# A long convolution by FFT and a gated causal unit on one core: second half in order of n, new evictions, and written-out queues

## The chip, the core and the metric

The kernel runs on one core of a Trainium2 chip. The core's engines run side by side, each with its own in-order queue, and meet at semaphores. PE is TensorE (matmuls; PEld its weight loads), DVE is VectorE, ACT is ScalarE, POOL is GpSimd and SP is SyncE, which here only issues DMA transfers. SBUF is the working memory of 128 partitions. PSUM takes the matmuls' results: eight banks of 512 float32 values per partition, used here as four tiles of two banks. The metric is the device time of one execution in microseconds.

## The reference

Input x is 8 batches of 3200 positions (n) by 256 channels in float32. Each batch is filtered along the positions by a complex filter, channel by channel, and then goes through a gated unit with a causal convolution of five taps:

```
X = np.fft.rfft(x, axis=1)
Y = X * (filt_r + 1j * filt_i)[None, :, :]
y = np.fft.irfft(Y, n=3200, axis=1)
gate_pre[n] = sum(conv_w[k] * y[n - 4 + k] for k in range(5))    # zeros before n = 0
out = (sigmoid(gate_pre) * (y @ w_val)) @ w_out
```

## The kernel before

**The transform.** A position is written n = 32a + r, with a from 0 to 99 and r from 0 to 31. Eight chunks of a batch hold four values of r each, with a on the partitions. Per batch the work is this, with the helper and its line:

1. `load_x` (L161, POOL): a chunk of x comes in as bfloat16. `s1` (L417, PE): a transform over a by one matrix of cosines and sines. `so` (L408 on ACT or L410 on DVE): eviction from PSUM.
2. `turn` (L436, DVE): four transposes of 32x32 blocks put r on the partitions (tile tt).
3. `s2` (L446, PE): the transform over r, 13 frequency slots in seven groups u. `xs`: eviction. `zed` (L464, DVE): two products, with the filter's real part (za) and imaginary part (zb). `inva` (L477, PE): the inverse over r. `ue`: eviction to u.
4. `wr` (L498) and `lv` (L508, L509, both SP): u goes to a scratch tensor in DRAM (escr) and comes back as vt, with the frequency on the partitions. `ib` (L518, PE): the inverse over a, in eight chunks. `ye` (L528, ACT): scaled eviction into yt, the filtered signal of a batch. Its columns are ordered by r, then a.

**The gated unit**, eight chunks of four r (400 columns) per batch, channels on the partitions: `halo` (L535, L537, POOL) fills the four columns ahead of r = 0. `conv` (L545, PE): five taps as 64x64 diagonal matrices; four matmuls, of two row groups and two column groups, belong to each tap, and each row group r writes PSUM bank r. `gate` (L554, ACT): sigmoid. `val` (L563, PE): y times w_val. `gv` (L573, DVE): their product. `outp` (L583, PE): times w_out, eight matmuls for four groups of 100 positions. `oe`: eviction to o. `store` (L597, L598, SP): two DMAs, of 96 and of 4 partitions.

**The start.** POOL generates index tables, issues batch 0's eight chunks of x and then 32 transfers of the two filters (L222, L225, L228), which fill half of the partitions of fr_t and fi_t. SP copies them to the other half by eight DMAs (L253). DVE and ACT compute the transform tables.

**What sets the order.** A planner (`Plan`, L30) holds every step as a task with its engine or engines, an assumed cost, its dependences and the buffers that it takes and gives back. It keeps a clock per engine, and among the tasks that could start it takes the one of the lowest rank, a number written for each task from its batch and its step. The result is the order in which each engine's queue is issued. Copies from PSUM may go to ACT or DVE, whichever the planner finds. Buffers: four PSUM tiles, ten chunks of x, one so, two tt, four u, four vt, two yt, three o.

Of the kernel before, what the change touches and what calls it, by code (L numbers as in the profile page):

```python
# [8 lines left out]
FP32 = mybir.dt.float32  # L9
# [7 lines left out]
L = 100  # L17
# [3 lines left out]
NV = 4 * NS  # L21
RC = 4
NCH = R // RC
UCH = [(m, min(2, NM - m)) for m in range(0, NM, 2)]
ICH = [NCH - 1] + list(range(NCH - 1))
MAGIC = 12582912.0


class Plan:
# [3 lines left out]
    def __init__(self, room, stay=1.0):  # L33
        self.tasks, self.room, self.stay = {}, dict(room), stay

    def add(self, name, engines, rank, deps, emit, take=(), give=(), land=0.0, mode=None):
        self.tasks[name] = dict(engines=engines, rank=rank, deps=deps, emit=emit, take=take,
                                give=give, land=land, mode=mode)

    def run(self):  # L40
        left = dict(self.tasks)
        users, need = {}, {}
        for n, t in left.items():
            need[n] = len(t["deps"])
            for d in t["deps"]:
                users.setdefault(d, []).append(n)
        ready_at = {n: 0.0 for n in left}
        free = {}
        mode = None
        gives = []  # L50
        ready = {n for n in left if need[n] == 0}
        order = []
        now = 0.0
        while left:
            gives.sort()
            while gives and gives[0][0] <= now + 1e-9:
                for pool in gives.pop(0)[1]:
                    self.room[pool] += 1
            best = None
            for n in ready:  # L60
                t = left[n]
                if ready_at[n] > now + 1e-9:
                    continue
                if any(self.room[p] < 1 for p in t["take"]):
                    continue
                for e, cost in t["engines"].items():
                    if free.get(e, 0.0) <= now + 1e-9:
                        away = e == "PE" and t["mode"] != mode
                        key = (t["rank"] + (self.stay if away else 0.0), cost)
                        if best is None or key < best[0]:  # L70
                            best = (key, n, e, cost)
            if best is None:
                later = [ready_at[n] for n in ready if ready_at[n] > now + 1e-9]
                later += [v for v in free.values() if v > now + 1e-9]
                later += [g[0] for g in gives if g[0] > now + 1e-9]
# [665 lines left out]
```

## Time and profile before

| | |
|---|---|
| median of 3 runs | 348.83 us (344.46 to 350.54) |
| the profiled execution's own time | 346.47 us |
| its span, first to last instruction | 344.8 us |
| busy: PE, DVE, ACT, POOL | 288.3, 256.4, 267.8, 68.0 us |
| mean granted TensorE clock | 0.97 |
| moved by DMA | 70.91 MB, mean 206 GB/s |

The profile is of one execution. The table of busy time gives each engine's busy time, its share of the span and the number of its instructions. The slices cut the span into 40 parts of 8.6 us; a digit is the busy share in tenths. The groups are instructions of one line, engine and shape. The chain of waits follows the work that ended last back to its releasers. A matmul's duration contains its way through the array, so the step from one start to the next is the better price of a matmul in a dense stretch.

### The profile page before, as it was taken

The page shows a single profiled execution, that of the slowest core. Times are in us where ns is not written, and L with a number is a line of the kernel's source. Part 1 is how long each engine was busy: PE and PEld are TensorE (multiplying, and loading weights), DVE is VectorE, ACT ScalarE, POOL GpSimd, SP SyncE. Part 2 cuts the span into 40 slices and gives each one's busy share as a digit, 9 for nine tenths or more (in the row PEclk, how much of TensorE's full clock was granted, in tenths as well). Part 3 has the DMA queues.
Part 4 walks back from the last instruction along what each step waited for, and adds up shares of the span by engine and source line. Part 5 has one row for each costly group of instructions (what it writes and reads, how often), then busy time and mean ns, then how long its engine had stood idle before and what let it go on. Part 6 is the DMA issues. An engine that isn't in the chain of part 4 may idle for free.

```text
span 344.8 us, 9785 instructions
## 1 busy us (share of the span) xinstructions
PE 288.3 (84%) x3988; PEld 191.6 (56%) x3988; DVE 256.4 (74%) x340; ACT 267.8 (78%) x309; POOL 68.0 (20%) x142
## 2 busy tenths in 40 slices
PE   2634677639999987999779997999999999999992
PEld 0023031326667755776457764776577677766762
DVE  4985477938698996889849994989798999734541
ACT  3954286928898987898849986998999789887663
POOL 8687455210112112110211011100100000001000
PEclk9999999969999999899989998999999999999997
DMA  6999999995899989898869969795677568778544
GB/s 95 155 168 163 213 192 195 206 238 168 199 232 247 272 233 231 245 229 251 170 200 207 271 176 250 214 245 171 199 208 221 156 204 261 234 214 248 160 144 143
DMA packets 57421, 70.91 MB, mean 206 GB/s; under 512 B 8608, under 2 KB 37152, under 8 KB 57376
## 3 DMA queue, kind: packets, MB, share of 16 engines
q1 hardware_dynamic: 45344, 55.20, 53.4%
q0 software_dynamic: 12032, 15.08, 29.0%
q8 instruction: 31, 0.51, 0.6%
q14 instruction: 14, 0.11, 0.1%
HBM read 43.78 MB, written 39.85 MB: 243 GB/s over the span
## 4 chain that ended last, share of the span: by engine, by line
PE 43%; DMA 24%; DVE 15%; ACT 7%; issue 4%; POOL 4%; SPq 1%; ACTq 0%; POOLq 0%; DVEq 0%
DMA vt<-escr 13%; PE ps L583 12%; PE ps L545 10%; DMA xt<-in_x_dram 6%; PE ps L563 6%; DVE tt L436 5%; DVE gv L573 5%; PE ps L417 5%; PE ps L518 5%; PE ps L477 4%; DMA fi_t<-in_filt_i_dram 3%; PE ps L446 3%; ACT o L408 2%; DVE xs L410 2%; POOL xt L161 2%
## 5 line engine op out<-in xcount | busy, mean ns | idle before, releaser
L573 DVE TENSOR_TENSOR gv<-ps,gt 128x800 bf16<-128x800 f32 x64 | 62.7, 980 | 19.9 <-PE ps L563 13.6
L408 ACT ACTIVATE o<-ps 100x1024 f32<-100x1024 f32 x59 | 61.0, 1035 | 16.9 <-PE ps L583 12.9
L410 DVE CAST xs<-ps 128x1024 bf16<-128x1024 f32 (+1 forms) x44 | 50.4, 1145 | 29.0 <-PE ps L446 29.0
L583 PE MATMUL ps<-wo_t,gv 128*100 128x256 bf16 x512 | 68.7, 278 | 2.7 <-DVE gv L573 1.1
L545 PE MATMUL ps<-yt,dg_t 64*64 64x400 bf16 x1280 | 67.3, 339 | 0.3
L408 ACT ACTIVATE so<-ps 128x1024 bf16<-128x1024 f32 x53 | 54.5, 1029 | 15.9 <-PE ps L417 11.1
L528 ACT ACTIVATE yt<-ps 128x800 bf16<-128x800 f32 x64 | 53.9, 846 | 15.9 <-PE ps L518 15.7
L583 PEld LDWEIGHTS <-gv 128*100 128x100 bf16 x512 | 54.5, 125 | 18.6 <-DVE gv L573 9.0
L161 POOL DMA_DIRECT2D xt<-in_x_dram x64 | 35.4, 556 | 124.5 <-PE ps L417 119.8
L554 ACT ACTIVATE gt<-ps 128x800 bf16<-128x800 f32 x64 | 54.1, 847 | 6.5 <-PE ps L545 5.3
L417 PE MATMUL ps<-xt,cf_t 100*128 100x512 bf16 x128 | 47.5, 462 | 12.2 <-DMA xt<-in_x_dram 11.2
L563 PE MATMUL ps<-yt,wv_t 128*128 128x400 bf16 x256 | 54.4, 335 | 0.5 <-ACT gt L554 0.5
L408 ACT ACTIVATE u<-ps 128x1024 bf16<-128x1024 f32 (+1 forms) x46 | 44.9, 982 | 7.2 <-PE ps L477 6.6
L518 PE MATMUL ps<-ci_t,vt 104*128 104x100 f16 x512 | 34.3, 212 | 16.5 <-DMA vt<-escr 16.4
L518 PEld LDWEIGHTS <-vt 104*128 104x128 bf16 x512 | 29.6, 100 | 30.1 <-DMA vt<-escr 19.8
L545 PEld LDWEIGHTS <-dg_t 64*64 64x64 bf16 x1280 | 34.5, 108 | 17.3 <-issue 4.2
L436 DVE STREAM_TRANSPOSE tt<-so 128x1024 f32<-128x1024 f32 x32 | 40.6, 1272 | 3.2 <-ACT so L408 3.2
L464 DVE TENSOR_TENSOR za<-xs,fr_t 128x1024 bf16<-128x1024 bf16 (+1 forms) x56 | 36.1, 649 | 1.4 <-ACT xs L408 0.2
L464 DVE TENSOR_TENSOR zb<-xs,fi_t 128x1024 bf16<-128x1024 bf16 (+1 forms) x56 | 35.5, 640 | 1.4 <-DMA fi_t<-in_filt_i_dram 1.4
L477 PE MATMUL ps<-zb,b_t 64*64 64x256 bf16 x416 | 29.7, 294 | 4.4 <-DVE zb L464 4.4
L477 PE MATMUL ps<-za,a_t 64*64 64x256 bf16 x416 | 30.3, 298 | 2.4 <-DVE za L464 2.1
L446 PE MATMUL ps<-tt,w_t 64*64 64x256 bf16 x416 | 24.2, 305 | 9.0 <-DVE tt L436 4.4
(93 smaller groups left out, 181.9 us busy)
## 6 DMA issues: line engine op xcount, KB each, us to landing
out_dram<-o SPq DMA_DIRECT2D x64, 384.0 KB
xt<-in_x_dram POOLq DMA_DIRECT2D x64, 200.0 KB, 6.7
escr<-u SPq DMA_DIRECT2D x48, 256.0 KB
vt<-escr SPq DMA_DIRECT2D x64, 192.0 KB
escr<-u SPq DMA_DIRECT2D x8, 128.0 KB
vt<-escr SPq DMA_DIRECT2D x64, 16.0 KB
out_dram<-o SPq DMA_DIRECT2D x64, 16.0 KB
fr_t<-in_filt_r_dram POOLq DMA_DIRECT2D x8, 56.0 KB, 4.7
```

The costliest lines, as they stand in the source:

```text
L408: nc.scalar.activation(dst, src, AF.Copy, **kw)
L410: nc.vector.tensor_copy(dst, src)
L417: nc.tensor.matmul(ps[:, 512 * h:512 * h + 512], lhsT=cf_t[0:L].rearrange("p h c i -> p (h c i)"), rhs=xv[:, DQ // 2 * h:DQ // 2 * h + DQ ...
L436: nc.vector.transpose(dst, src)
L464: (nc.vector if e == "DVE" else nc.gpsimd).tensor_tensor(z[:, :, 0:nm * D], xs_[:, :, 0:nm * D], f[:, :, m0:m0 + nm, :].rearrange("p h m d ...
L477: nc.tensor.matmul(ps[64 * h:64 * h + 64, 512 * t + D * a:512 * t + D * a + D], lhsT=tab[rows, h, m0 + a, :], rhs=zz[w][rows, h, D * a:D * ...
L518: nc.tensor.matmul(ps[:, o:o + L], lhsT=v[0:NV, a, 128 * dh:128 * dh + 128], rhs=ci_t[0:NV, :], start=True, stop=True)
L545: nc.tensor.matmul(ps[64 * dh:64 * dh + 64, 512 * r:512 * r + RC * L], lhsT=dg_t[rows, dh, k, :], rhs=y[rows, dh, RC * j + k:RC * j + k + ...
L554: nc.scalar.activation(g[...], ps[:, :].rearrange("p (h n) -> p h n", h=2)[:, :, 0:RC * L], AF.Sigmoid)
L563: nc.tensor.matmul(ps[:, 512 * eh:512 * eh + RC * L], lhsT=wv_t[:, dh, 128 * eh:128 * eh + 128], rhs=y[:, dh, H + RC * j:H + RC * j + RC, ...
L573: nc.vector.tensor_tensor(gv_[...], ps[:, :].rearrange("p (h n) -> p h n", h=2)[:, :, 0:RC * L], g[...], op=ALU.mult)
L583: nc.tensor.matmul(ps[0:L, D * a:D * a + D], lhsT=gv_[:, eh, L * a:L * a + L], rhs=wo_t[:, eh, :], start=(eh == 0), stop=(eh == 1))
```

## The change

- **Order of n.** `ye` writes yt in order of n: it reads a chunk from PSUM with r and a exchanged and writes runs of four values. The gated unit then works on seven blocks of consecutive positions: six of 512 and one of 128. A block's conv waits for all eight chunks of its batch. `halo` is one memset. `outp` takes groups of 128 positions; so that each partition holds four consecutive rows of the output, `gv` reads its inputs at every fourth column and writes them in groups. `store` is one DMA of 128 partitions, except for the last full block, whose gv, oe and store are split in two.
- **Convolution.** Its matmuls write bank dh for channel half dh, from both row groups. In batches 6 and 7 two blocks of 512 are computed together by 32x32 tiles, 80 matmuls for the pair, in two PSUM tiles; the channels come out rotated, so w_val and w_out are held with rotated copies.
- **Filters.** One tile f_t holds both parts. POOL issues 24 transfers in place of 32, and eight copies on DVE (seven) and ACT (one) fill the other half in place of SP's eight DMAs. `zed` is one product of both parts in place of two.
- **Batch 0** has no way through DRAM: `pad` clears the rest of u, and `back` transposes u into vt on DVE in four pieces. A second inverse matrix (ci_t) fits its order of rows.
- **Buffers.** One tt, one u (a whole batch), one vt (a whole batch), four o. PSUM is one tile of four slots, and the plan names each task's slot.
- **Queues.** The order of each engine is a list of task numbers in the kernel; the planner only runs it to find slots and the order between engines. `warm` fills gaps that the planner sees on PE between 14 and 45 us with matmuls whose results nobody reads.
- **Smaller edits.** The taps' diagonal matrices are made by ACT in ten instructions, and w_val and w_out come in two steps.

The core of the diff:

```diff
-    NVB, NGB, NOB = 4, 3, 3
+TURN = (0,)
+SMALL = (6, 7)
...
+            for e, line in lines.items():
+                if line and free.get(e, 0.0) <= now + 1e-9 and can(line[0]):
+                    begin(line.pop(0), e)
...
+    ps_all = pp.tile([128, 4, 1024], FP32, name="ps")
...
-                    for h in range(2):
-                        nc.gpsimd.dma_start(
-                            out=dst[p:p + 16, h, m0:m1, :].rearrange("p m d -> p (m d)"),
-                            in_=fsrc(f, k + NS * h, [[100 * D, 16], [1, nm * D]]))
+                    nc.gpsimd.dma_start(
+                        out=dst[p:p + 16, :, m0:m1, :].rearrange("p h m d -> p h (m d)"),
+                        in_=fsrc(f, k, [[100 * D, 16], [NS * D, 2], [1, nm * D]]))
...
-        for m0, m1 in FCUT:
-            for dst in (fr_t, fi_t):
-                for t in range(2):
-                    p = 64 * t
-                    nc.sync.dma_start(out=dst[p + 32:p + 64, :, m0:m1, :],
-                                      in_=dst[p:p + 32, :, m0:m1, :])
...
+    def warm(us):
+        flat = w_t[...].rearrange("p s k -> p (s k)")
+        ps = psum()
+        for h in range(int(us / WARM)):
+            o = 512 * (h % 2)
+            nc.tensor.matmul(ps[:, o:o + 512], lhsT=flat[:, 0:128],
+                             rhs=flat[:, o + 128:o + 640], start=True, stop=True)
...
+    def twin(half, w, t, e):
+        m0, m1 = FCUT[half]
+        p = 64 * t
+        copy(e, f_t[p + 32:p + 64, w, :, m0:m1, :], f_t[p:p + 32, w, :, m0:m1, :])
...
+    def zed(b, u):
...
+        nc.vector.tensor_tensor(
+            z[:, :, :, 0:nm * D],
+            st.pop(("XS", b, u))[:, :, 0:nm * D].unsqueeze(1)
+            .to_broadcast((128, 2, 2, nm * D)),
+            f_t[:, :, :, m0:m0 + nm, :].rearrange("p w h m d -> p w h (m d)"), op=ALU.mult)
...
+    def pad(b):
+        st["U", b] = upool.tile([128, 32, D], BF16, name="u")
+        if b in TURN:
+            nc.gpsimd.memset(st["U", b][:, NS:32, :], 0.0)
...
+    def back(b, q):
+        if q == 0:
+            st["V", b] = vpool.tile([128, R, D], BF16, name="vt")
+        src, dst = (t_[:, :, DQ * q:DQ * q + DQ].bitcast(FP32).rearrange("p s w -> p w s")
+                    for t_ in (st["U", b], st["V", b]))
+        nc.vector.transpose(dst, src)
...
-            y[:, :, p0:p0 + RC, :].rearrange("p h a n -> p h (a n)"),
-            ps[:, :].rearrange("p (h n) -> p h n", h=2)[:, :, 0:RC * L],
+            y[:, :, H:H + N].rearrange("p h (a r) -> p h a r", r=R)[:, :, :, RC * j:RC * j + RC],
+            ps[:, :].rearrange("p (h n) -> p h n", h=2)[:, :, 0:RC * L]
+            .rearrange("p h (r a) -> p h a r", r=RC),
...
+        if not pair(b, c):
+            ps = psum()
+            for k in range(K):
+                for r, dh in ((0, 0), (1, 0), (0, 1), (1, 1)):
+                    rows = slice(64 * r, 64 * r + 64)
+                    o = 64 * (r ^ dh)
+                    nc.tensor.matmul(ps[o:o + 64, 512 * dh:512 * dh + w],
+                                     lhsT=dg_t[rows, dh, k, :],
+                                     rhs=y[rows, dh, BLK * c + k:BLK * c + k + w],
+                                     start=(k == 0), stop=(k == K - 1))
+            st["cv", b, c] = ps
+            return
+        two = [psum(0), psum(1)]
+        for k in range(K):
+            for n in range(4):
+                dh, s = n // 2, n % 2
+                p = BLK * (c + s) + k
+                for i in range(4):
+                    rows = slice(32 * i, 32 * i + 32)
+                    o = 32 * ((i + n) % 4)
+                    nc.tensor.matmul(two[s][o:o + 32, 512 * dh:512 * dh + BLK],
+                                     lhsT=dg_t[rows, dh, k, 32 * (i % 2):32 * (i % 2) + 32],
+                                     rhs=y[rows, dh, p:p + BLK],
+                                     start=(k == 0), stop=(k == K - 1))
...
-            for r, dh in ((0, 0), (1, 1), (0, 1), (1, 0)):
-                rows = slice(64 * r, 64 * r + 64)
-                nc.tensor.matmul(ps[64 * dh:64 * dh + 64, 512 * r:512 * r + RC * L],
...
+        if w == BLK:
+            o = o.rearrange("p h (r q) -> p h r q", r=RC)
+            i0, i1 = (t_.rearrange("p h (q r) -> p h r q", r=RC) for t_ in (i0, i1))
...
-                nc.tensor.matmul(ps[0:L, D * a:D * a + D],
-                                 lhsT=gv_[:, eh, L * a:L * a + L], rhs=wo_t[:, eh, :],
+                nc.tensor.matmul(ps[:, D * a:D * a + D],
+                                 lhsT=gv_[:, eh, 128 * a:128 * a + 128], rhs=wo_t[:, c % 2 * pair(b, c), eh, :],
...
-    plan = Plan(dict(ps=4, xt=NXT, so=1, t=2, xs=3, za=3, zb=3, u=4, e=2, v=NVB, y=2, g=NGB,
-                     gv=NGB, o=NOB))
+    plan = Plan(dict(xt=NXT, so=1, t=1, xs=3, z=3, u=1, e=2, v=1, y=2, g=NGB, gv=NGB, o=NOB), 4, QUEUES)
...
+                if slots and COLD[0] < idle and at < COLD[1] and at - idle > WARM:
+                    warm(at - idle)
```

610 lines of the change are left out of this document (344 added, 266 removed), and 70 rows, old and new, of tables (ACT, DVE, PE, POOL).

## The prediction, made before the changed kernel had run

> **What bounds the kernel now.** I read the busy table and the forty slices first, then the busy time by stage, then the chain that ended last for the weak stage, then the timeline of TensorE (PE) for the prices of a dense stage.
>
> ```profile
> PE 288.3 (84%) x3988; PEld 191.6 (56%) x3988; DVE 256.4 (74%) x340; ACT 267.8 (78%) x309; POOL 68.0 (20%) x142
> PE   2634677639999987999779997999999999999992
> DMA  6999999995899989898869969795677568778544
> ```
>
> No engine is far from full, and PE stands at 9 from slice 9 (78 us) almost to the end. The loss lies before it.
>
> ```profile
> 0.00:45.00 45.00, 22.49 (x178) 8.15 (x178) 30.47 (x81) 24.14 (x28) 31.36 (x69) 1.00 0.95 160
> 45.00:78.00 33.00, 20.72 (x244) 9.99 (x242) 21.89 (x29) 21.38 (x25) 12.18 (x23) 0.90 1.04 210
> 78.00:220.00 142.00, 129.68 (x1886) 90.90 (x1879) 115.06 (x130) 119.77 (x140) 20.40 (x41) 0.96 0.87 222
> 220.00:330.00 110.00, 106.94 (x1604) 77.01 (x1603) 85.06 (x98) 95.88 (x112) 4.02 (x10) 1.00 0.73 211
> ```
>
> Busy time by stage: columns PE, weight loads, DVE, ACT, POOL, then granted clock, DMA share, GB/s. Up to 78 us only 420 of 3988 matmuls run, while DMA is full. Much of that PE time is slow work: the first-stage matmul has these durations from 30 to 60 us, and from 220 us on.
>
> ```profile
> L417 PE MATMUL ps<-xt,cf_t x26: 606/628/632, 35.5 to 59.8; 100*128 100x512 bf16 x26
> L417 PE MATMUL ps<-xt,cf_t x22: 382/384/395, 221.1 to 264.0; 100*128 100x512 bf16 x22
> ```
>
> The recorded clock says 1.00 in both places, but two such matmuls step by 1.03 us early and by 0.45 late, so PE ran at half rate. The chain shows what the first batch waited for (start, us, what):
>
> ```profile
> 34.36 11.60 DMA xt<-in_x_dram
> ...
> 63.07 11.63 DMA vt<-escr
> ...
> 74.75 0.85 PE ps L518 x8
> ```
>
> PE's in-order queue held batch 0's inverse behind batch 1's input, and then the reload through DRAM came in at 74.7 us. The second stage needs a PE price list. In the timeline (start, us) the steps between starts are 0.91 for a projection of eight matmuls (L583), 0.68 for val (L563), 0.45 for one inverse chunk (L518), 0.97 for a conv block (L545).
>
> ```profile
> 301.59 0.52 PE L518 MATMUL ps<-ci_t,vt 104*128 104x100 f16 x8
> 302.04 1.04 PE L545 MATMUL ps<-yt,dg_t 64*64 64x400 bf16 x20
> 303.01 1.08 PE L583 MATMUL ps<-wo_t,gv 128*100 128x256 bf16 x8
> 303.92 0.84 PE L563 MATMUL ps<-yt,wv_t 128*128 128x400 bf16 x4
> 304.60 0.52 PE L518 MATMUL ps<-ci_t,vt 104*128 104x100 f16 x8
> ```
>
> With 0.45 for L417's pair, 0.15 for a frequency slot of L446 and 0.26 for one of L477, the whole program is 64x0.91 + 64x0.68 + 64x0.97 + 64x0.45 + 64x0.45 + 104x0.41 = 264 us. By 78 us, 48 matmuls of L417, 104 of L446, 200 of L477 and 16 of L518 had run: 22 us of it. The other 242 took 264 us (78 to 342): a fill of **0.92**; 2.8 us of last store follow.
>
> **The change, part by part.**
>
> *PE in the dense stage.* Rows in order of n give 25 groups of 128 per batch in place of 32 of 100: 400 projection matmuls in place of 512, 50x0.91 = 45.5 against 58.2, so -12.7. Val streams the same columns: 48x0.87 + 8x0.22 = 43.5, no change. Conv: 0.97 is five passes of 400 columns (0.17 each, val's rate) and 0.12 beside them. At 512 columns that is 5x0.218 + 0.12 = 1.21, 36 times; the 128-column rest 0.39, 8 times. No row has 32x32 tiles. A pair of blocks costs between 1.21 (sixteen tiles in one pass, as L545's four are) and 2.42 (nothing gained). Sixteen weight loads per pass weigh on it: L335 at half rate shows four in 0.107 us, so up to 0.43 for sixteen against 0.218. I take 1.4, nearer to L545's row, six times. Conv is then 43.6 + 3.1 + 8.4 = 55.1 against 62.1, -7.0. Odd offsets of the moving operand have no row; bounds none to a doubled pass, none taken, since every aligned row here streams at the column rate. PE needs 264 - 20 = **244 us**.
>
> *ACT and DVE.* By start-to-start steps (0.92 to 0.94 for 1024 columns on ACT, 1.14 on DVE, 0.72 for 800 on ACT, 0.90 on DVE) I count from the two lists of instructions: ACT 257 before and 253 after, DVE 249 and 249. Sixteen fewer evictions of o (64 to 48, and 8 small) give 12, one product of 2048 columns in place of two of 1024 (1.13 to 1.21 against 1.21) gives 3, fewer gates 1. The filter copies cost it back: seven on DVE, one on ACT. The nearest rows are 0.60 for 1024 and 1.03 for 1664 columns, so 0.5 to 1.6 each for 3072 to 3584; I take 0.9 on DVE, 3 on ACT. The back-transposes cost 4 steps of 1.16 (tt's row) to twice that, since words lie 512 B apart; I take 1.7. So these engines gain nothing, and at 231 us of PE after the start they need about 220 and 210: the cover is thin.
>
> Two operations lose their contiguous rows. gv reads PSUM and the gate at every fourth element, and yt is written in runs of four with PSUM read 100 words apart. The nearest rows are gv's 980 ns for 800 contiguous columns, and tt, whose words stand two apart, 1272 ns for 1024: both about 1.2 ns per column. So I take gv at 0.90 + 224x1.04 = 1.13 a step, with twice that as upper end (+54 us of DVE).
> The Trainium skill, Vector Engine (DVE) Microarchitecture Reference, section 5.2, speaks against this part: a source that hops at every element is given 1.73 to 2.5 ns per column, against 1.05 for pairs of adjacent words. It measured that in SBUF on 4-byte words; tt's row moves single words at full speed but only two words apart, so no run here decides it. By the page gv would be 1.8 to 2.6 us, +32 to +69 us of DVE, and the end about 317 to 357 us.
>
> *The start.* POOL issues 24 filter transfers in place of 32; the last one left at 28.7 and took up to 5.4. Eight issues of 0.51 are 4 us at most, none if the DMA engines (0.98 full there) are the limit: landing at 29 to 33. SP's eight duplicates go. Behind the last landing stand two copies (1.8), four products (4.6), an inverse slot pair and its eviction (1.5), four back-transposes (6.8). Batch 0's inverse starts at 44 to 48 instead of 74.7. The warming matmuls (at 14 to 45 us) use idle PE; where the plan's gap isn't there they cost up to 0.43 each and delay what stands behind them, a few us, but hold the rate that L417 lacked. I take **47 us** as start of the dense stage. Done by then: two batches of L417 (7.2), one of L446 and L477 (5.3): 12.5.
>
> *Buffers and queues.* tt, u and vt are single now. A batch's u must be written out before the next is filled; in a batch time of 31 us the chain u, DRAM, vt (12 us at 63 to 75) fits. Conv waits for all eight pieces of its batch, 8x0.72 on ACT; other batches' matmuls stand beside it in PE's queue. SP loses 56+8 second stores; POOL's halo copies (8 us) were off the path.
>
> *Sum.* (244 - 12.5) / 0.92 = 251.6; 47 + 251.6 + 2.8 = 301.4 span. What lies around the span is 346.47 - 344.8 = 1.7: 303.1, against the profiled execution's own 346.47. The median of the runs is 348.83, 1.007 of it: **305 us**.
>
> **Rivals.**
>
> *The transfers set the pace* (0.18). The kernel moves 70.9 MB; without batch 0's round trip (3.4) and the duplicates (1.7) 65.8, some 58 of them after 47 us. In 250 us that is 232 GB/s; the stages above gave 222 and 211. For it: PE and its weight loads waited 36 us for vt. Against: 30 us from 100 on ran at 247. At 222 GB/s the end is 47 + 262 + 4.5, 316 us on the median's scale; at 205 (the rate of 160 to 280) 338.
>
> *A fuller stage* (0.20). From 220 to 330 the fill by the same prices is 0.98; the two low stages of the clock come after idle vt waits. At 0.97: 47 + 239 + 4.5, 292; with a start at 44, 289. Against it: ACT and DVE need 0.9 all the way.
>
> *gv at twice a contiguous step* (0.05). DVE is the bound: 210 + 54 at 0.92, its share from 100 to 130, gives 47 + 287 + 4.5: 341 us. From about 1.6 us a step DVE is later than PE.
>
> *Row tiles in one bank take turns* (0.05), the case that ends slower. In L545 before, row group r writes bank r. After, both row groups write bank dh at once, four of them in a pair. If those can't overlap, a block needs a second pass (36x1.09 + 8x0.27) and a pair three more (6x3.3): +61 us of PE, 318 for the stage, 372 us. It is slower by 2% if over 46 of these 61 come. Against it: the partitions written are different ones.
> The Trainium skill, TensorEngine Tiling (Array Packing), Gotcha 1, has that rule: different row tiles cannot access the same PSUM bank simultaneously. No run so far shows a pass of this form.
>
> *It doesn't do what it says* (0.01): batch 0 still waits for DRAM; the two instruction lists show that its reload is gone.
>
> **How the numbers follow.** The forecast (295 to 316) has 0.51. Two per cent is about what can be told from no change here. Faster by over 2% (below 341.9) hold the forecast, the fuller stage, the transfers and half of gv: 0.91; the same 0.04; slower 0.05. The range 288 to 335 leaves out the row tiles, gv, and the ends of the fuller stage and of the transfers.
>
> **What would show it.** Right: first L518 near 45; 400 projection matmuls at 0.11 step; a 512-column block at 1.2, a pair at 1.2 to 1.6; gv near 1.2 in duration; PE at 9 from slice 6. Wrong: gv over 1.5, a block over 2, vt or xt first among PE's waits, or ACT and DVE under 0.85 with PE waiting for evictions.

## The result and the profile after

| | before | after |
|---|---|---|
| median | 349.69 us (344.46 to 353.29, 4 runs) | 308.97 us (304.47 to 313.84, 4 runs) |
| ratio | | 0.8815, 95% interval 0.854 to 0.909 |
| the profiled execution: time, span | 346.47, 344.8 us | 306.64, 304.8 us |
| busy PE, DVE, ACT | 288.3, 256.4, 267.8 us | 269.7, 258.5, 260.7 us |
| moved by DMA | 70.91 MB | 65.99 MB |

A second group of runs of the unchanged new kernel gave 309.1 us and a tighter ratio, 0.8853 (0.8804 to 0.8902). The forecast was 305. Some executions of a kernel take over 1.5% longer than its fastest; ratios and their intervals leave those out and medians count them, so a ratio need not equal the quotient of two medians.

From the page of the kernel after, the busy table, one line of slices (7.6 us each) and the transfers:

```profile
PE 269.7 (88%) x3980; PEld 161.5 (53%) x3980; DVE 258.5 (85%) x287; ACT 260.7 (86%) x308; POOL 61.8 (20%) x122
PE   2885986779998999779999997899999999999992
DMA packets 53017, 65.99 MB, mean 217 GB/s; under 512 B 7728, under 2 KB 34224, under 8 KB 52976
```

PE is far busier before 45 us, but 14.7 us of that are the 56 warming matmuls. After it the row dips to 6, 7, 7 (slices 6 to 8) and stands mostly at 9 only from slice 9 on, 69 us. I had expected it from slice 6. Three engines now stand at 85 to 88%.

Busy time by stage of the kernel after (stretch, length, then PE, weight loads, DVE, ACT, POOL with instruction counts, granted clock, DMA share, GB/s):

```profile
0.00:47.00 47.00, 34.25 (x296) 14.01 (x297) 41.79 (x85) 35.65 (x49) 35.31 (x68) 1.00 0.89 133
47.00:63.50 16.50, 11.71 (x172) 7.63 (x171) 14.72 (x14) 16.41 (x21) 7.57 (x14) 0.90 0.91 141
63.50:78.00 14.50, 13.28 (x220) 7.33 (x212) 13.04 (x12) 13.67 (x17) 1.77 (x4) 1.00 0.81 191
78.00:190.00 112.00, 103.17 (x1456) 61.25 (x1452) 100.11 (x93) 101.75 (x117) 16.86 (x33) 0.98 0.88 235
190.00:290.00 100.00, 98.11 (x1712) 64.96 (x1711) 80.77 (x78) 87.23 (x103) 0.31 (x3) 1.00 0.71 245
290.00:304.80 14.80, 9.17 (x140) 6.28 (x138) 8.12 (x10) 6.00 (x7) 0.00 (x0) 0.92 0.66 258
```

Between 47 and 63.5 us ACT is busy 16.41 of 16.5: it, not PE, sets the pace there. From 78 to 190 the three engines are level (103, 100, 102 of 112). Only from 190 on does PE alone lead (98 of 100).

The timeline says what PE and ACT do in that early stretch (start, duration, what). First PE's, of the kernel after:

```profile
48.98 4.06 PE L658 MATMUL ps<-ci_t,vt 128*128 128x100 f16 x55 [1.64 <-DVE vt L648]
...
63.50 1.27 PE L697 MATMUL ps<-yt,dg_t 64*64 64x512 bf16 x20
```

Then ACT's, of the same kernel:

```profile
46.07 3.76 ACT L538 ACTIVATE so<-ps 128x1024 bf16<-128x1024 f32 x4
49.69 5.24 ACT L667 ACTIVATE yt<-ps 128x800 bf16<-128x800 f32 x7
55.01 1.02 ACT L538 ACTIVATE xs<-ps 128x1024 bf16<-128x1024 f32 x1
55.93 2.85 ACT L538 ACTIVATE so<-ps 128x1024 bf16<-128x1024 f32 x3
...
60.48 0.87 ACT L667 ACTIVATE yt<-ps 128x800 bf16<-128x800 f32 x1
```

Seven of the eight chunks of batch 0's second inverse run at 47 to 53 us, as forecast, and the eighth at 56.6. But a block's convolution needs all eight pieces of yt, and ACT writes seven of them up to 55 and the eighth from 60.5 to 61.3, with ten evictions for the other batches ahead of them and between. The first convolution starts at 63.5.

Late in the kernel the timeline gives the prices (step from start to start):

```profile
262.04 1.35 PE L711 MATMUL ps<-yt,dg_t 32*32 32x512 bf16 x80
263.32 0.40 PE L731 MATMUL ps<-yt,wv_t 128*128 128x128 bf16 x4
...
264.93 1.05 PE L762 MATMUL ps<-wo_t,gv 128*128 128x256 bf16 x8
265.81 0.52 PE L658 MATMUL ps<-ci_t,vt 104*128 104x100 f16 x8
266.17 1.03 PE L731 MATMUL ps<-yt,wv_t 128*128 128x512 bf16 x4
267.04 0.52 PE L658 MATMUL ps<-ci_t,vt 104*128 104x100 f16 x8
```

A pair of blocks steps by 1.28 us, eight projection matmuls by 0.88, val by 0.87, an inverse chunk by 0.36 here. The step of a single block depends on what stands next in PE's queue, in the kernel after:

```profile
152.21 1.25 PE L697 MATMUL ps<-yt,dg_t 64*64 64x512 bf16 x20
153.29 0.28 PE L607 MATMUL ps<-z,a_t 64*64 64x256 bf16 x4
...
155.50 1.27 PE L697 MATMUL ps<-yt,dg_t 64*64 64x512 bf16 x20
156.71 0.62 PE L547 MATMUL ps<-xt,cf_t 100*128 100x512 bf16 x2
```

Before tiled matmuls (64x64 or 32x32) it steps by 1.08, before untiled ones by 1.18 to 1.21. A block of 400 in the kernel before steps by 0.87 (48 of 64) or by 0.95 to 0.97. An inverse chunk steps by 0.45 before tiled and by 0.36 before untiled matmuls in both kernels; 50 of 64 have a tiled neighbour before, 13 after.

Waits of PE in the kernel after, the two longest and the first for DVE (us in total, times, longest):

```profile
PE ps L658 <- DMA vt<-escr: 6.6, 6, 1.8
PE ps L547 <- DMA xt<-in_x_dram: 5.9, 3, 5.5
PE ps L607 <- DVE z L592: 2.6, 3, 2.1
```

With the weight loads' own 8.2 us, the waits for vt fell from 36.2 to 14.8 us; one wait of 5.5 for xt is the very first load.

**PE's work in one count.** To compare kernels I price PE's work by its columns alone. In dense stretches of both kernels a pass over 512 columns steps by 0.216 us (five passes of 400 in 0.843, five of 512 in 1.079), and tiles that run at once count once. The changes between tiled and untiled matmuls, about 0.1 us each, are left out; there are 140 before and 136 after. Each matmul's start tells how much of the work lies before a point, and so the fill of a stretch. Four of the runs described below are listed too.

| PE's work by columns, us | total | done by 47 us | done by 78 us | fill, 47 us to the last matmul | fill, 78 us to the last matmul |
|---|---|---|---|---|---|
| before | 235.1 | 9.6 | 19.2 | 0.77 | 0.83 |
| after | 216.6 | 11.1 | 30.8 | 0.81 | 0.84 |
| b0_dram | 216.6 | 11.1 | 20.4 | 0.78 | 0.84 |
| greedy (with 27 matmuls that its trace lacks) | 216.6 | 10.7 | 26.7 | 0.72 | 0.74 |
| greedy_lead | 216.6 | 11.1 | 26.9 | 0.78 | 0.81 |
| all_back | 235.1 | 11.1 | 24.5 | 0.82 | 0.87 |

This count leaves out small parts that the forecast's prices hold, so 0.83 here stands for its 0.92. From 78 us on the fill stayed (a second trace of the kernel after, from the run again, has 0.83). The last matmul ends at 300.3 us instead of 338.9. Of these 38.6 us, at the old fill, 18.5 us less work is worth 22, and 11.6 us more done by 78 us is worth 14; the fill itself brings the other 2.

### The profile page after: what moved, and what is told of

Same layout as the page of the kernel before. It is cut to its first block, busy times and chain, and to the rows that moved or that the text cites. A ratio compares the mean times of both kernels' runs of the same rounds, so it can differ in the third digit from the quotient of the medians.

```text
span 304.8 us, 9446 instructions
## 1 busy us (share of the span) xinstructions
PE 269.7 (88%) x3980; PEld 161.5 (53%) x3980; DVE 258.5 (85%) x287; ACT 260.7 (86%) x308; POOL 61.8 (20%) x122
## 2 busy tenths in 40 slices
DMA packets 53017, 65.99 MB, mean 217 GB/s; under 512 B 7728, under 2 KB 34224, under 8 KB 52976
## 5 line engine op out<-in xcount | busy, mean ns | idle before, releaser
L752 DVE TENSOR_TENSOR gv<-ps,gt 128x1024 bf16<-128x1024 f32 (+1 forms) x49 | 58.3, 1197 | 17.1 <-PE ps L731 11.9
L592 DVE TENSOR_TENSOR z<-xs,f_t 128x2048 bf16<-128x2048 bf16 (+1 forms) x56 | 63.3, 1139 | 1.4 <-ACT xs L538 1.1
L721 ACT ACTIVATE gt<-ps 128x1024 bf16<-128x1024 f32 (+1 forms) x56 | 51.3, 940 | 8.0 <-PE ps L711 4.9
L762 PE MATMUL ps<-wo_t,gv 128*128 128x256 bf16 x400 | 51.9, 273 | 1.5 <-DVE gv L754 1.2
L731 PE MATMUL ps<-yt,wv_t 128*128 128x512 bf16 (+1 forms) x224 | 53.0, 360 | 0.1
L697 PE MATMUL ps<-yt,dg_t 64*64 64x512 bf16 (+1 forms) x880 | 48.4, 348 | 0.7 <-ACT so L538 0.4
L762 PEld LDWEIGHTS <-gv 128*128 128x128 bf16 x400 | 37.0, 98 | 13.3 <-issue 3.9
L658 PE MATMUL ps<-ci_t,vt 104*128 104x100 f16 (+1 forms) x512 | 33.6, 217 | 10.2 <-DMA vt<-escr 6.6
L538 ACT ACTIVATE xs<-ps 128x1024 bf16<-128x1024 f32 (+1 forms) x40 | 38.8, 984 | 4.1 <-PE ps L576 3.5
L566 DVE STREAM_TRANSPOSE tt<-so 128x1024 f32<-128x1024 f32 x32 | 38.1, 1224 | 3.5 <-ACT so L538 3.1
L538 ACT ACTIVATE o<-ps 128x1024 f32<-128x1024 f32 (+2 forms) x35 | 34.3, 983 | 6.3 <-PE ps L762 4.1
L731 PEld LDWEIGHTS <-wv_t 128*128 128x128 bf16 x224 | 18.9, 98 | 19.2 <-issue 5.3
```

Source lines behind the costliest of these rows:

```text
L538: nc.scalar.activation(dst, src, AF.Copy, **kw)
L566: nc.vector.transpose(dst, src)
L592: nc.vector.tensor_tensor(z[:, :, :, 0:nm * D], st.pop(("XS", b, u))[:, :, 0:nm * D].unsqueeze(1) .to_broadcast((128, 2, 2, nm * D)), f_t[ ...
L658: nc.tensor.matmul(ps[:, o:o + L], lhsT=v[rows, RC * j + a, 128 * dh:128 * dh + 128], rhs=ci_t[rows, way, :], start=True, stop=True)
L697: nc.tensor.matmul(ps[o:o + 64, 512 * dh:512 * dh + w], lhsT=dg_t[rows, dh, k, :], rhs=y[rows, dh, BLK * c + k:BLK * c + k + w], start=(k ...
L721: nc.scalar.activation(g[:, :, 0:w], two_banks(ps, w), AF.Sigmoid)
```

## Experiments

Each ran beside fresh runs of the kernel before on the same chip. Where two runs are of different chips I compare their ratios, and give a difference on 348 us.

| run | what | median, us | before there, us | ratio, 95% interval |
|---|---|---|---|---|
| again | the changed kernel | 309.1 | 347.73 | 0.8853 (0.8804 to 0.8902) |
| no_pair | single blocks in batches 6, 7 | 315.17 | 347.73 | runs scatter, none given |
| pad_outp | 512 projection matmuls again | 315.75 | 347.73 | 0.9072 (0.9036 to 0.9107) |
| b0_dram | batch 0 through DRAM | 317.12 | 347.73 | 0.9020 (0.8963 to 0.9078) |
| pad_late | the repeats in batches 4 to 7 alone | 314.29 | 345.57 | 0.9069 (0.8976 to 0.9163) |
| no_warm | without warming matmuls | 310.52 | 345.57 | 0.8989 (0.8914 to 0.9063) |
| greedy | order by the earlier rule | 340.69 | 345.57 | 0.9897 (0.9847 to 0.9946) |
| start_only | before, with the new start | 342.54 | 345.57 | 0.9931 (0.9887 to 0.9976) |
| greedy_lead | greedy, transforms ahead | 319.15 | 347.61 | 0.9236 (0.9193 to 0.9280) |
| all_back | b0_dram, no_pair and pad_outp in one | 327.06 | 347.61 | 0.9454 (0.9401 to 0.9507) |
| pair567 | batch 5 paired too, new queues | 306.40 | 347.61 | 0.8856 (0.8808 to 0.8905) |
| before_lead | before, transforms ahead | 344.61 | 346.17 | 1.0048 (0.9982 to 1.0114) |

The traces of these runs can be compared batch by batch. "Batches 0 to 3" is the time from the first convolution of batch 0 to that of batch 4, "batches 4 to 7" from there to the last matmul.

| trace | first convolution at, us | batches 0 to 3, us | batches 4 to 7, us |
|---|---|---|---|
| before | 79.1 | 142.9 | 116.9 |
| after | 63.5 | 148.1 | 88.7 |
| again | 64.3 | 150.8 | 88.7 |
| b0_dram | 75.2 | 147.6 | 88.7 |
| no_warm | 65.5 | 146.2 | 88.7 |
| no_pair | 65.4 | 147.7 | 94.6 |
| pad_outp | 64.2 | 149.4 | 95.0 |
| pad_late | 66.3 | 149.2 | 94.3 |
| all_back | 69.8 | 149.5 | 100.9 |
| pair567 | 65.5 | 145.5 | 89.0 |
| greedy | 62.0 | 161.9 | 109.3 |
| greedy_lead | 62.4 | 155.6 | 93.3 |
| before_lead | 82.3 | 150.9 | 106.1 |

The last column repeats to 0.1 us wherever PE's work there is the same, so it shows what a part is worth late in the kernel far more sharply than whole times do. PE is busy 87.1 of these 88.7 us. The middle column differs by some 3 us between two executions of one kernel. Against the kernel before, batches 0 to 3 take some 5 us longer and batches 4 to 7 28 us less: the last first-stage matmul runs at 208 us, ahead of batch 4's first convolution (211.6), and in the kernel before at 264, behind it (222.0).

### again: the changed kernel once more

> The changed kernel once more, beside the three that follow, as their yardstick: 305 to 312 us, with its conv blocks of 512 columns at 1.08 us a step and its pairs at 1.28. Nothing is told apart by it alone.

It gave 309.1 us (306.48 to 311.34), and is the reference for the rest.

### no_pair: the paired convolution undone

```diff
-SMALL = (6, 7)
+SMALL = ()
```

The odd blocks' convolutions stand right behind the even ones in PE's queue.

> The twelve blocks of batches 6 and 7 are convolved one by one with 64x64 tiles; each pair in PE's queue is replaced by its two blocks, side by side. If PE sets the pace there, as I count it, six times (2 x 1.08 - 1.28) = 5.3 us come back: the changed kernel's time plus 5 to 6. Rival, ACT's gates set the pace of the last two batches: plus 0 to 1.

+6.1 us by the medians on the same chip, but its six executions lie between 309.15 and 320.68, too far apart for an interval, and the lowest is as fast as the changed kernel. The trace decides: its batches 4 to 7 take 94.6 us instead of 88.7, 5.9 more. Six pairs save 6 x (2 x 1.08 - 1.285) = 5.3 us of PE; what they save is the bound at that point. The rival (0 to +1) falls.

### pad_outp and pad_late: projection matmuls added back

```diff
-        for a in range(width(c) // 128):
+        for a in [0] + list(range(width(c) // 128)):                     # pad_outp
+        for a in ([0] if b > 3 else []) + list(range(width(c) // 128)):  # pad_late
```

The first group of each block is computed twice with the same result.

> Every projection computes its first group of 128 rows twice, so that PE has 512 of these matmuls again, as before the change; nothing else differs. 112 x 0.109 = 12.2 us more on PE. If the fewer projection matmuls were worth their full price: plus 12 to 13. Rival, evictions on ACT and DVE set the pace and PE had room: plus 0 to 5.

> The changed kernel with the first pair of output matmuls of each block issued twice in batches 4 to 7 alone: 56 more matmuls of 0.109 us, 6.1 us of PE. With the repeat in all eight batches the time rose 6.65 us for 12.2 us of PE. Theory: TensorE ends the wait only in the second half (windows: busy 98 of 100 us between 190 and 290, against 25 of 31 and 103 of 112 before that), so this half alone costs nearly all of the 6.65: +5 to +6.1, 314 to 315. Rival, each repeat costs half its time wherever it stands: +3.3, 312. Rival 2, the early half paid: +0 to +2.

112 repeats are 12.2 us of PE and cost 7.6 by the ratios ((0.9072 - 0.8853) x 348, with an uncertainty of about 2), 6.65 by the medians: between theory and rival. The 56 in batches 4 to 7 alone, 6.1 us of PE, come to the same ratio (0.9069, +7.5 us with an uncertainty of about 4). The traces are sharper: batches 4 to 7 take 95.0 and 94.3 us instead of 88.7, that is 6.3 and 5.6 more. So the late repeats cost about their full time, and the early ones nothing that stands out of the 3 us by which executions differ there. That fits the stages above: PE is alone at the bound only after 190 us.

### b0_dram: batch 0's way through DRAM

```diff
-TURN = (0,)
+TURN = ()
```

Batch 0's `wr` and `lv` come first in SP's queue, its `ib` and `ye` directly ahead of its first convolution and gate.

> Batch 0 goes through DRAM like the others, its inverse moved behind batch 1's first stages in the queues of PE and ACT, the four back-transposes (7.4 us of DVE) left out. If the early start of batch 0's second half is worth what I count, its first inverse comes at 58 to 70 us instead of 47, and the time grows by 8 to 15. Rival, PE has enough other work from batches 1 and 2 in that stretch: plus 0 to 3.

First inverse at 63.1 us instead of 47.1, first convolution at 75.2 instead of 63.5, and +5.8 us by the ratios ((0.9020 - 0.8853) x 348, with an uncertainty of about 2.6): less than the theory's 8 to 15 and more than the rival's 0 to 3. The medians differ by 8.0, the figure that later expectations use. One stage of its profile, of an execution of 318.08 us, in the columns of the table above:

```profile
47.00:78.00 31.00, 17.79 (x204) 9.37 (x208) 16.30 (x14) 19.18 (x22) 8.59 (x17) 0.65 0.83 168
```

PE is busy 17.8 us there against 25.0 in the changed kernel, at a recorded clock of 0.65. By 78 us 20.4 us of its columns are done, against 30.8 in the changed kernel. So an inverse that is 16 us later costs 10.4 us of PE's work at that point, less than 16 since the changed kernel itself has no convolution before 63.5 us, and about 6 at the end. Its batches 4 to 7 take the same 88.7 us. Where a part of the loss is won back isn't shown.

### no_warm: no matmuls on constants

```diff
-                    warm(at - idle)
+                    pass
```

> The changed kernel without the 56 matmuls on constants between 17.4 and 45.2 us (14.7 us of busy PE in its trace). The sum counted them as idle time of PE. Theory: no change to +3 us (309 to 312); the first inverse still starts near 47, since the four transposes in front of it are VectorE's and wait for the last z and its inverse at 38.7 to 39.6; what changes is the clock recorded in the first 60 us, and single steps of the first transform and inverse. Rival 1, the warm matmuls hold back batch 0's real work on the one queue: faster by 1 to 3 us. Rival 2, without them the dense stage begins at half clock, as the run with batch 0 through DRAM showed between 47 and 78 us (0.65 recorded, and 8 us lost, part of it there): +4 to +8.

```profile
0.00:47.00 47.00, 23.46 (x238) 11.06 (x239) 40.39 (x85) 33.65 (x43) 33.59 (x64) 0.96 0.84 126
```

The ratio is 0.0136 higher, 4.7 us with an uncertainty of about 3: in rival 2's range (+4 to +8), but the theory (0 to +3) isn't excluded. Rival 1, a gain, falls. The stage shows what the warming holds: the real matmuls up to 47 us take 23.5 us of busy PE for 10.7 us of columns, against 34.25 - 14.7 = 19.6 for 11.1. The first inverse moves from 47.1 to 49.1. Rival 2's reason, a dense stage at half clock, isn't seen: the recorded clock from 47 to 78 us is 0.89 against 0.94. But the profiled execution was the fastest of its six (306.81), so it can't show where the others lose more.

### greedy: the earlier rule in place of the queues

```diff
-            for e, line in lines.items():
-                if line and free.get(e, 0.0) <= now + 1e-9 and can(line[0]):
-                    begin(line.pop(0), e)
+            for n in waiting:
+                for e, cost in t["engines"].items():
+                    if free.get(e, 0.0) <= now + 1e-9:
+                        key = (rank(n) + (1.0 if away else 0.0), cost)
...
```

The task of the lowest key begins, among those that could start. The ranks are those of the kernel before, with the step between blocks stretched from eight to seven per batch.

> The changed kernel with all its tasks, costs and buffers, but the written-out queues replaced by a choice at planning time: the ready task of the lowest number (chunk by chunk, the numbers that the kernel before used, with its charge of 1 for a change of tile shape). The sum gave the order no term of its own: it took the share filled of the stage, 0.92, over from the kernel before, that is, held that the written-out order is worth nothing by itself. If so: 306 to 314, as the changed kernel. Rival, the order carries a part of the gain: half the distance to the kernel before or more, 325 to 345. Between the two, 315 to 325, the order is worth 6 to 16 us and the parts that I priced are worth that much less.

340.7 us: the rival holds, and fully. With the earlier rule the whole change is worth one per cent; against this rule, whose numbers nobody tuned for the new blocks, the queues carry 36 us ((0.9897 - 0.8853) x 348). Stages and waits of PE of this run:

```profile
47.00:78.00 31.00, 22.37 (x293) 13.64 (x294) 27.65 (x23) 24.34 (x28) 5.75 (x11) 0.83 0.74 141
78.00:190.00 112.00, 97.02 (x1340) 56.88 (x1348) 94.31 (x87) 90.44 (x106) 14.16 (x28) 0.97 0.85 230
190.00:290.00 100.00, 89.95 (x1236) 53.70 (x1244) 78.99 (x74) 79.12 (x90) 3.76 (x10) 0.97 0.65 204
```

```profile
PE ps L671 <- ACT yt L641: 9.1, 5, 2.0
...
PE ps L632 <- DVE vt L622: 5.8, 2, 3.3
```

L671 is the convolution in that file, L641 the eviction to yt. All engines are lower in every stage. PE's fill is 0.74 from 78 us on, against 0.84, with the same columns. Its longest named wait is the convolution's for the eight pieces of yt, 9.1 us in five waits of up to 2.0, which I had costed at nothing because "other batches' matmuls stand beside it in PE's queue". In the written-out order they do once batch 0 is past, and this wait is not among PE's waits above 0.4 us; in the earlier rule's order they don't. The last first-stage matmul runs at 257 us, the last inverse chunk at 313.5.

### greedy_lead: how much of that is running ahead

```diff
+    lead = 0.0 if k in ("dg", "tp", "te", "fd") or not b else float(b) * NCH
+    ahead = (0.15 if k in ("lx", "s1", "so", "t", "pd", "s2", "xs", "z", "ia", "ue", "wr", "k", "lv") else
+             0.10 if k in ("ib", "ye", "ha") else 0.0) * lead
...
-        return t0 + j
+        return t0 + j - ahead
```

> The changed kernel with its order chosen by the earlier rule, but with the numbers of the transforms (loads, stages 1 and 2, filter, first inverse, and their transfers) lowered by 0.15 of 8 per batch, and those of the second inverse by 0.10 of 8 per batch: the transforms of batch 7 come 8.4 places earlier against the dense blocks, those of batch 0 not at all. Under the earlier rule the last first-stage matmul ran at 257 us and the last dense matmul at 333; under the written-out order at 208 and 300. Theory: what the written-out order brings is chiefly that the transforms run ahead, so that dense blocks are left to fill PE at the end; then this rule gains about half of the order's 36 us, 320 to 330. Rival, it is the fine order of single tasks, queue by queue: no gain, 337 to 344. Rival 2, running ahead alone is nearly all of it: 306 to 316.

319.2 us: 23 of the 36 come back ((0.9897 - 0.9236) x 348), a little more than the theory's half. The last first-stage matmul moves from 257 to 216 us (208 in the written-out order), and the fill from 78 us from 0.74 to 0.81. Two numbers per batch do that; the other 13 us are left for the fine order of single tasks.

### before_lead: the same numbers in the kernel before

```diff
+        if m:
+            rank = rank - NCH * b * (0.10 if kind in ("ib", "ye", "ha") else 0.15)
```

> The kernel before, nothing of the change in it, but its rule's numbers lowered as in the run with transforms ahead: loads, stages 1 and 2, filter, first inverse and their transfers by 0.15 of 8 per batch, the second inverse by 0.10 of 8. Theory: an order in which the transforms run ahead is worth something on any amount of work, as the written-out order with three parts taken back was (ratio 0.945): here 0.95 to 0.975, 330 to 339, less than there since it has neither blocks of 512 nor the fine order. Rival, it needs the changed kernel's buffers and shorter queues (one vt buffer loaded whole, four gate buffers): 0.985 to 1.01. Rival 2, the earlier kernel loses, since its first batch starts late and what runs ahead only waits for it: above 1.01.

Nothing, as the first rival had it, within one per cent. The order did change: the last first-stage matmul moved from 264 to 243 us, the last inverse chunk from 330 to 315. But the last projection stayed at 339. What batches 4 to 7 won (106.1 us instead of 116.9) batches 0 to 3 lost (150.9 instead of 142.9), and the first convolution came 3 us later. PE's work isn't the limit here: all_back has the same 235.1 us of columns and ends 19 us earlier. The rival's own reason, buffers and queues, wasn't tested.

### start_only: the kernel before with the new start

```diff
-                    for h in range(2):
-                        nc.gpsimd.dma_start(
-                            out=dst[p:p + 16, h, m0:m1, :].rearrange("p m d -> p (m d)"),
+                    nc.gpsimd.dma_start(
+                        out=dst[p:p + 16, :, m0:m1, :].rearrange("p h m d -> p h (m d)"),
...
-                    nc.sync.dma_start(out=dst[p + 32:p + 64, :, m0:m1, :],
-                                      in_=dst[p:p + 32, :, m0:m1, :])
...
+        copy(e, f[p + 32:p + 64, :, m0:m1, :], f[p:p + 32, :, m0:m1, :])
...
+        nc.vector.transpose(dst, src)
```

The transposes stand for batch 0's `wr` and `lv`. Its u takes one of the two tt buffers and its vt one of the two yt buffers. Four filter copies are on DVE and four on ACT.

> The kernel before with the changed start alone: batch 0 turned back on VectorE instead of passing through DRAM, the filter's first copies by VectorE and ScalarE instead of 8 transfers on SyncE, 24 instead of 32 transfers for the filter; the chunks of 400, the convolution in 64x64 tiles and the rule that chooses the order stay. By the sum's terms the dense stage starts 31 us earlier with some 10 us less of its work done before: (242 + 10) / 0.92 = 274 us from 47, a span of about 324 and a time of 326, that is 20 to 22 us under the kernel before. Rival 1, what the run with batch 0 through DRAM suggests (an inverse 16 us later costs 8): half of it, 335 to 339. Rival 2, the order is the gain: the rule used before spends the earlier start on the wrong tasks: 344 to 350.

-2.4 us, not -20: the theory and rival 1 both fall, and the time lies in rival 2's range. The first inverse came at 66.2 us instead of 74.8, not at 47. Here are PE's longest wait and a piece of DVE's timeline in this run, and then DVE's timeline in the changed kernel:

```profile
PE ps L457 <- DVE tt L447: 22.6, 2, 15.9
```

```profile
22.40 0.95 DVE L421 COPY fr_t<-fr_t 32x3072 bf16<-32x3072 bf16 x1
23.36 0.95 DVE L421 COPY fi_t<-fi_t 32x3072 bf16<-32x3072 bf16 x1
24.33 0.69 DVE L421 CAST a_t<-ps 128x512 f16<-128x512 f32 x1
25.03 1.25 DVE L447 STREAM_TRANSPOSE tt<-so 128x1024 f32<-128x1024 f32 x1
...
33.32 1.25 DVE L447 STREAM_TRANSPOSE tt<-so 128x1024 f32<-128x1024 f32 x1
```

```profile
17.38 4.62 DVE L566 STREAM_TRANSPOSE tt<-so 128x1024 f32<-128x1024 f32 x4 [2.15 <-ACT so L538]
22.03 5.82 DVE L540 COPY f_t<-f_t 32x3072 bf16<-32x3072 bf16 x4
```

The rule put the inverse's table ahead of the four transposes of batch 0, and filter copies and table evictions among them. They ended at 34.6 instead of 22.0; PE stood for 15.9 us behind them. The written-out order puts the transposes first. So some 12 of the 19 us by which the first inverse comes later than in the changed kernel are an effect of order: the parts only make the early start possible. The second wait of this line, 6.7 us up to 60.0, is for batch 1's transposes, which alternate with batch 0's back-transposes on DVE. Whether the order or the borrowed buffers put them there isn't separated.

### all_back: three parts taken back, the new order kept

The edits of b0_dram, no_pair and pad_outp in one kernel.

> The changed kernel's written-out order with three of its parts taken back together: batch 0 through DRAM, no paired convolution, and the first pair of output matmuls of every block issued twice (512 again). Blocks of 512 points, the filter's copies on engines and the order of all other tasks stay. One by one these cost +8.0, +6.1 and +6.65. The run with the earlier rule in place of the order came out at a ratio of 0.990, that is, with the order gone these parts were worth next to nothing; the question is what the order is worth with the parts gone. Theory A, they add up: 309 + 20.7 = 330, a ratio near 0.945, so that the order (with 512-point blocks) is worth some 19 us even on nearly the old amount of work. Theory B, order and parts need each other: well above the sum, 338 to 348 (0.97 to 1.0). Theory C, they overlap, since a late start gives the other two their slack: 320 to 325.

0.9454, 21 us above the changed kernel, with an uncertainty of about 2.5: theory A. The three runs alone add up to 20.75 by medians, and to 5.8 + 6.1 + 7.6 = 19.5 with the ratios where there are any. The traces add up too: batches 4 to 7 take 88.7 + 5.9 + 6.3 = 100.9 us by the parts, and 100.9 measured. In the new order the parts add up; in the old one they and all the rest were worth 1%.

The remaining 19 us stand on the old amount of work: this kernel has the same 235.1 us of columns as the kernel before. Its first inverse is at 62 us instead of 75, so that 5.3 us more are done by 78 us, worth about 6; from there its fill is 0.87 instead of 0.83, worth about 13. The order isn't alone in that: blocks of 512, the single filter product, the filter copies on engines and the other buffers are in this kernel too.

### pair567: one more paired batch

```diff
-SMALL = (6, 7)
+SMALL = (5, 6, 7)
```

A pair needs two of four PSUM slots at once, so the queues were set anew.

> The changed kernel with the convolution of batch 5 paired in 32x32 tiles too, and the queues set anew for it (a pair needs two PSUM slots at once). PE's list gets shorter by 3 x (2 x 1.08 - 1.285) = 2.6 us in a stretch that the repeats of output matmuls in batches 4 to 7 showed to be PE's (they cost about their full time). Theory: -1 to -3 us, a ratio of 0.877 to 0.883. Rival: the pairs take two of four slots in the stretch where the transforms of batch 7 still run beside them, and the wait for slots takes the gain: 0 to +4 us.

No gain that can be seen: 0.8856 (0.8808 to 0.8905) against 0.8853, the lower end of the rival; the uncertainty of about 2.4 us leaves room for a small one. The trace agrees: batches 4 to 7 take 89.0 us against 88.7, and batch 5 itself 25.9 against 25.7. So 2.6 us less of PE bought nothing there, though 6 us more in the same batches cost about 6. The pair task also moved others in the queues, so a loss by order isn't separated from a lack of gain. No version beat the changed kernel by more than the runs can tell.

## Why the prediction was right, and where it was not

The time was right, and the range held it. Step by step it looks different:

- **"By 78 us ... 22 us of it" and the start at 47.** The start of the first inverse, forecast at 44 to 48, was 47.1 to 49.0; done by 47 were 12.5 us by the forecast's prices, as forecast, and the four back-transposes step by 1.82 us (1.7 taken). But "start of the dense stage" was wrong by 16 us: the first convolution needs all of yt, which ACT, busy 16.41 of 16.5 us, had written only at 61.3, and ran at 63.5. The step that failed is that the eight evictions (8 x 0.72) stood in the text and got no time in the sum, nor did the ten for other batches that stand among them. The sum has 12.5 + 0.92 x 31 = 41 us done by 78 us against 22 before, worth 21 us; by columns it was 30.8 against 19.2, worth 14. And an inverse 16 us later (b0_dram) cost 5.8, where the sum gives 16.
- **PE's list, 244.** Its fall by 20 us came: 18.5 by columns, 12.1 of them in the projection (12.7 forecast) and 6.4 in the convolution (7.0). A reading was wrong, not the sum: the 0.12 beside five passes belongs to the change to an untiled neighbour. A block of 400 steps by 0.97 there and by 0.87 otherwise, so the 264 counts it in every block, before and after alike. A pair's passes of sixteen tiles step by 0.217, as those of four do, and its 1.285 (1.4 taken) contains such a change; the sixteen weight loads that I put at up to 0.43 per pass don't show.
- **Fill 0.92, carried over.** It held, but nothing in the prediction stood behind it. The reading itself was a little low: it counts to 342 us, where the last matmul of the kernel before ended at 338.9. By columns the fill from 78 us is 0.83 before and 0.84 after; between 47 and 78 us, where the sum had it too, it is 0.64. It isn't a property of the machine: the same tasks in the earlier rule's order have 0.74. PE's work fell by 8% and ACT's and DVE's not at all (busy 260.7 and 258.5 after, 267.8 and 256.4 before), so three engines are nearly level. I gave the order of the queues no term and no rival; it decides 36 us, nearly as much as the whole gain. That the new queues kept the old fill was luck, as far as the prediction goes. The profiled execution took 306.64 us where the sum gave 303.1: the start brought 7 us less than its share, and smaller terms gave half of that back.
- **ACT and DVE gain nothing.** Right, -7 and +2 us busy. "The cover is thin" was right too: they stand at 0.92 and 0.89 from 47 to 190 us (131.8 and 127.9 of 143).
- **gv at 1.13 a step.** Measured 1.14, in a duration of 1219 ns for 1024 columns. From the page of the kernel after, with the eviction to yt below it (busy us, mean ns of one, idle before):

```profile
L752 DVE TENSOR_TENSOR gv<-ps,gt 128x1024 bf16<-128x1024 f32 (+1 forms) x49 | 58.3, 1197 | 17.1 <-PE ps L731 11.9
L667 ACT ACTIVATE yt<-ps 128x800 bf16<-128x800 f32 x64 | 51.6, 846 | 10.0 <-PE ps L658 9.9
```

  A copy of 1024 contiguous columns takes DVE 1221 ns, and the eviction to yt took 846 ns before the change too. So reading every fourth column costs nothing visible, and neither does yt's writing in runs of four. By the figures of the Trainium skill, Vector Engine (DVE) Microarchitecture Reference, section 5.2, the estimate for gv was 1.8 to 2.6 us; this case's trace doesn't agree for a bfloat16 and a PSUM operand read at every fourth element.
- **Row tiles in one bank.** They don't take turns: 1.08 us is the column rate of five single passes, and the sixteen tiles of a pair's pass start 3 to 9 ns apart. The Trainium skill's rule in TensorEngine Tiling (Array Packing), Gotcha 1, does not show for tiles that write different partitions of a bank.
- **A fuller stage.** Only from 190 us on: 0.89 by columns from 190 to 290, but 0.79 from 78 to 190, where ACT and DVE are the "0.9 all the way" that I had put against it. (The stretch from 220 to 330 us before, which this rival went by, has 0.87.)
- **Transfers set the pace.** No: 65.99 MB moved (65.8 forecast), 235 to 245 GB/s in the dense stages, PE's waits for vt down by 21 us. Still vt is first among PE's waits (6.6 us), which I had named as a sign of being wrong; as a sign it was badly chosen, since a first place says nothing of its size.
- **Buffers and queues, SP, POOL.** The single buffers were counted as free. The reloads into the single vt waited 5.8 us, in three waits, for the last use of the old one (SP's waits); what that costs PE isn't shown. PE waited 1.7 us for tt. The warming, counted as free or a small loss, was worth some 5 us, with an uncertainty of 3.

What stays open is why removing PE work late bought nothing (pair567) when adding it cost its full time, which share of the order's remaining 13 us lies in which queue, and what the new buffers and blocks of 512 alone are worth.

## What to carry to other kernels

A fill measured before a change is a property of its order of work as much as of its engines: multiply by the old fill only if the queues are set anew, and give the order a rival of its own. Price two kernels alike before comparing their fills: a step read off a timeline contains what the next task adds to it. In a kernel whose engines are level, first let the stages that feed the others run ahead (two numbers gave 23 of 36 us here), and look at the order whenever a part that makes an earlier start possible brings nothing. A matmul removed can be worth its step only in stages where PE alone is at the bound: read that from the busy time by stage, and test it by repeating work there. That a repeat costs its time doesn't promise that a removal gains it.

## What the runs showed of the hardware

- Four 64x64 tiles, two of them in each PSUM bank, ran five passes of 512 columns in 1.08 us. Sixteen 32x32 tiles, four in each bank, step by 0.217 us per pass of 512 columns; five passes and the change to an untiled neighbour took 1.285 us.
- A change between tiled (64x64 or 32x32) and untiled matmuls cost about 0.1 us: a conv block of 512 columns steps by 1.08 before tiled and 1.18 to 1.21 before untiled matmuls, one of 400 by 0.87 and 0.95 to 0.97, an inverse chunk by 0.36 before untiled and 0.45 before tiled ones.
- A transpose of 32x32 blocks on VectorE with words 512 B apart in source and target took 1929 ns (median) for 1024 words per partition; the one on tt, with 1024 words two apart, 1224 ns on average.
- Without the warming matmuls the real PE work up to 47 us took 23.5 us of busy time instead of 19.6, at a recorded clock of 0.96 instead of 1.00: most of the slow rate is in the durations and hardly in the recorded clock.
- Copies within 32 partitions of 3072 and 3584 bfloat16 values took VectorE between 0.95 and 2.84 us (the median of seven is 1.09), one on ScalarE 2.76 us.
